# The first matmul of each lot of scores, values and transposes is kept behind everything traced on TensorE ahead of it

## The chip, the core and the metric

The kernel runs on one core of a Trainium2 chip, as one program. The metric is the time of one execution on the device in microseconds. The engines are TensorE (PE; its weight loads are listed apart as PEld), VectorE (DVE), ScalarE (ACT), GpSimd (POOL) and SyncE (SP), which issues the DMAs. Each works through its own list of instructions in order; semaphores hold it where it needs another engine's result.

## The reference

Four batches of 12480 tokens of 128 channels go through an attention over 49 agents, and the result through a feed-forward layer with the activation h cos h.

```python
def sm(a, b):
    s = scale * (a @ b.transpose(0, 2, 1))
    s = s - s.max(-1, keepdims=True)
    e = np.exp(s)
    return e / (e.sum(-1, keepdims=True) + 1e-09)
a2k = sm(agents, k)
agent_v = a2k @ v
q2a = sm(q, agents)
x = (q2a @ agent_v).reshape(B * S, D)
h = x @ w_in
g = h * np.cos(h)
return g @ w_out
```

## The kernel before

Tokens go in 52 groups of 960 (13 for each batch), a group in two halves of 480. For a batch, the agents' values are first multiplied into the 2048 columns of `w_in` (the tiles `a`, and `b1`, `b2` for a correction term), so that a half needs only the 49 weights of each token, turned (`pT`, 113 rows).

The **step loop** (L554) has 832 steps, 8 for each half. A step n multiplies `pT` by two blocks of `a` into `ph` (L562, two matmuls of 480 columns, a *`ph` pair* here), takes the cosine on ScalarE (`c`, L565), and forms (c - 1) h on VectorE (`r`, L567). Four steps later (`LAG`), two matmuls add `r` times `w_out` to the half's output `po` (L584, a *second-layer pair*). With the last step of a half come two correction matmuls (L580, L581) and ScalarE's copy of `po` to `osb` (L586). `ph` has three buffers, each of two PSUM banks.

Between them, by a plan (`plan`, `extra`, L455 to L550), run **lots** that prepare other groups and the next batch. Each stands, in the code, right behind the `ph` pair of its step and ahead of that step's second-layer pair:
- scores of queries or keys (L90): eight matmuls of 49 columns in fp32, each shown as two instructions, so 16 in a lot; then a copy to SBUF on ScalarE (L351, L173) or on VectorE, and a maximum on VectorE (L355, L184);
- values (L235): eight matmuls of 98 columns, 16 instructions; then a sum on VectorE (L240);
- transposes of a group's weights (L380): four; then a copy on ScalarE (`p`, L382), and casts and subtractions on GpSimd that make `pT` (L385, L386).

All lots and the outputs `po` take their PSUM tile from one pool, `one`, of two buffers: `po` holds one, the lots share the other, and when a half ends the two change places. A lot then waits for the copy to `osb` of the half before.

The order on each engine isn't that of the code. A scheduler lays it out ahead of time by its own estimate of when each instruction is ready, the code's order coming second; it may cut a lot into pieces and place them before or behind other pairs. `tc.keep_in_program_order(ins)` adds an edge without a wait: `ins` stays behind the last instruction traced before it on its engine. Before the change it is used for the first loads, for the bursts of exponentials and for one table load. Three times in a batch ScalarE does such a burst, with a table load before and after it.

## Time and profile before

| | |
|---|---|
| median of 3 runs | 1233.39 us (1231.19 to 1235.24) |
| the profiled execution's own time | 1232.16 us |
| its span on the core | 1230.4 us |
| matmuls busy | 1168.4 us |
| VectorE busy | 1074.3 us |
| ScalarE busy | 976.7 us |

Busy times are sums over the span, and the ends of matmuls are modelled, so that TensorE's price for a thing is better read from the distance between starts. What limits a stretch is read from that stretch.

### The profile page before, as it was taken

The page shows a single profiled execution, that of the slowest core. Times are in us where ns is not written, and L with a number is a line of the kernel's source. Part 1 is how long each engine was busy: PE and PEld are TensorE (multiplying, and loading weights), DVE is VectorE, ACT ScalarE, POOL GpSimd, SP SyncE. Part 2 cuts the span into 40 slices and gives each one's busy share as a digit, 9 for nine tenths or more (in the row PEclk, how much of TensorE's full clock was granted, in tenths as well). Part 3 has the DMA queues.
Part 4 walks back from the last instruction along what each step waited for, and adds up shares of the span by engine and source line. Part 5 has one row for each costly group of instructions (what it writes and reads, how often), then busy time and mean ns, then how long its engine had stood idle before and what let it go on. Part 6 is the DMA issues. An engine that isn't in the chain of part 4 may idle for free.

```text
span 1230.4 us, 17371 instructions
## 1 busy us (share of the span) xinstructions
PE 1168.4 (95%) x6349; PEld 963.1 (78%) x6349; DVE 1074.3 (87%) x1219; ACT 976.7 (79%) x1167; POOL 353.1 (29%) x389
## 2 busy tenths in 40 slices
PE   8999999999999999999999999999999999998997
PEld 7878888778887888878787888877878776776674
DVE  5898888988789889898889888888888999999997
ACT  2367788887778888788968888887887888888996
POOL 1211222633322213273412222137332323121220
PEclk9998999999999999999999999999999999998999
DMA  8973232224322232323231232322331110000001
GB/s 310 245 212 97 88 106 80 81 73 136 113 65 81 80 106 71 113 80 103 61 113 61 69 110 80 98 81 81 97 92 38 35 42 37 23 27 27 23 32 35
DMA packets 39190, 107.74 MB, mean 88 GB/s; under 512 B 4344, under 2 KB 4728, under 8 KB 39096
## 3 DMA queue, kind: packets, MB, share of 16 engines
q1 hardware_dynamic: 39096, 106.55, 27.6%
q8 instruction: 52, 0.85, 0.3%
q14 instruction: 42, 0.34, 0.1%
HBM read 80.97 MB, written 25.56 MB: 87 GB/s over the span
## 4 chain that ended last, share of the span: by engine, by line
PE 66%; DVE 16%; ACT 12%; issue 4%; DMA 2%; SPq 0%; ACTq 0%; DVEq 0%
PE ph L562 25%; PE one L584 18%; PE one L90 11%; DVE r L567 10%; ACT c L565 6%; PE one L235 5%; ACT osb L586 3%; PE one L580 2%; PE one L581 2%; DVE rz L364 1%; PE ph L98 1%; DMA raw<-w_out 1%; PE one L380 1%; ACT e L360 1%; DVE mx L355 1%
## 5 line engine op out<-in xcount | busy, mean ns | idle before, releaser
L567 DVE SCALAR_TENSOR_TENSOR r<-c,ph 128x960 fp32r<-128x960 f32 x832 | 923.8, 1149 | 96.1 <-ACT c L565 90.0
L565 ACT ACTIVATE c<-ph 128x960 f32<-128x960 f32 x832 | 795.9, 978 | 176.0 <-PE ph L562 150.3
L562 PE MATMUL ph<-pT,a 113*128 113x480 f32 x1664 | 544.9, 409 | 30.7 <-DVE r L567 21.5
L584 PE MATMUL one<-r,w 128*128 128x480 f32 x1664 | 515.0, 391 | 1.1 <-ACT osb L586 0.6
L562 PEld LDWEIGHTS ph<-pT,a 113*128 113x128 f32 x1664 | 287.1, 192 | 129.8 <-DVE r L567 56.9
L584 PEld LDWEIGHTS one<-r,w 128*128 128x128 f32 x1664 | 311.8, 192 | 47.3 <-ACT osb L586 1.5
L90 PEld LDWEIGHTS one<-ag,xt 128*120 128x120 f32 x1408 | 172.6, 186 | 36.8 <-ACT osb L586 26.0
L371 POOL TENSOR_TENSOR p<-e,rz 120x392 f32<-120x392 f32 x52 | 43.8, 847 | 486.6 <-PE one L380 403.1
L90 PE MATMUL one<-ag,xt 128*120 128x49 f32 x1408 | 172.2, 265 | 9.0 <-ACT osb L586 7.6
L386 POOL TENSOR_TENSOR pT<-p,pT 49x480 fp32r<-49x480 f32 x104 | 126.9, 1220 | 8.0
L385 POOL CAST pT<-p 49x480 fp32r<-49x480 f32 x104 | 60.8, 585 | 74.8 <-ACT p L382 52.4
L235 PEld LDWEIGHTS one<-s,vt 120*128 120x128 f32 x624 | 76.9, 192 | 6.5 <-ACT osb L586 2.6
L357 POOL TENSOR_TENSOR e<-e,mx 120x392 f32<-120x392 f32 x49 | 41.4, 844 | 131.5 <-DVE mx L355 126.3
L235 PE MATMUL one<-s,vt 120*128 120x98 f32 x624 | 77.4, 272 | 1.0 <-ACT osb L586 0.6
L586 ACT COPY osb<-one 128x480 f32<-128x480 f32 x104 | 57.6, 554 | 2.9 <-PE one L584 2.9
L224 POOL TENSOR_TENSOR es<-es,s 120x392 f32<-120x392 f32 x36 | 36.8, 1021 | 47.9 <-ACT s L216 45.6
L380 PEld LDWEIGHTS one<-ident,p 120*113 120x113 f32 x208 | 31.6, 178 | 12.2 <-ACT osb L586 7.2
L580 PE MATMUL one<-pT,b 113*128 113x480 f32 x104 | 41.0, 394 | 0.0
L581 PE MATMUL one<-pT,b 113*128 113x480 f32 x104 | 40.6, 390 | 0.0
L212 POOL TENSOR_TENSOR s<-s,mxb 120x1568 f32<-120x1568 f32 (+1 forms) x9 | 31.6, 3538 | 29.8 <-DVE mxb L208 29.8
L380 PE MATMUL one<-ident,p 120*113 120x120 f32 x208 | 37.4, 274 | 2.3 <-ACT osb L586 2.3
L382 ACT COPY p<-one 113x480 f32<-113x480 f32 x52 | 28.9, 556 | 6.3 <-PE one L380 6.3
(93 smaller groups left out, 532.9 us busy)
## 6 DMA issues: line engine op xcount, KB each, us to landing
xt<-qT SPq DMA_DIRECT2D x52, 480.0 KB, 3.5
vt<-v SPq DMA_DIRECT2D x104, 240.0 KB, 3.5
outT<-osb SPq DMA_DIRECT2D x51, 480.0 KB, 2.6
xt<-kT SPq DMA_DIRECT2D x46, 480.0 KB, 3.5
c<-kT SPq DMA_DIRECT2D x6, 480.0 KB, 5.7
raw<-w_in SPq DMA_DIRECT2D x8, 256.0 KB, 5.3
raw<-w_out SPq DMA_DIRECT2D x8, 256.0 KB, 6.8
outT<-osb SPq DMA_DIRECT2D x2, 240.0 KB, 2.8
```

Source lines behind the costliest of these rows:

```text
L90: nc.tensor.matmul(ps[:, t, :], xt[:, t * TT:(t + 1) * TT], ag[:, b, :], start=True, stop=True)
L235: nc.tensor.matmul(po, vt[:, t, :], twice(e[:, t, :]), start=(t == 0 and (g == 0 or not lone)), stop=(t == GT - 1 and (g == NG - 1 or not ...
L380: nc.tensor.transpose(pt[:KR, t * TT:(t + 1) * TT], p_in[n % 2][:, t, :KR], ident[:TT, :TT])
L385: nc.gpsimd.tensor_copy(pT[own, c], p[own])
L386: nc.gpsimd.tensor_sub(pT[other, c], p[own], pT[own, c].bitcast(F32))
L562: nc.tensor.matmul(ph[:, j, :CH], ai[:, f], pTs[q % 3][:, c], start=True, stop=True)
L565: nc.scalar.activation(cos, h, AF.Sin, bias=HALF_PI, scale=1.0)
L567: nc.vector.scalar_tensor_tensor(r, cos, 1.0, h, op0=ALU.subtract, op1=ALU.mult)
L580: nc.tensor.matmul(po, b1[k], pTs[q % 3][:, c], start=False, stop=False)
L581: nc.tensor.matmul(po, b2[k], pTs[q % 3][:, c], start=False, stop=False)
L584: nc.tensor.matmul(po, w1[:, f, :], r[:, j, :], start=(f == 0), stop=(f == NF - 1))
L586: nc.scalar.copy(osb[:, c * CH:(c + 1) * CH], po)
```

## The change

A list `ordered` switches on a helper `behind` while the step loop is traced. In it, the first matmul of each lot of scores, the first of each lot of values, and the first transpose of each lot is kept behind the last instruction traced on TensorE before it, which is the second matmul of the same step's `ph` pair. The other matmuls of a lot carry no edge.

```diff
--- before.py
+++ after.py
@@ -71,6 +71,12 @@
     fits = const.tile([KR, NB], F32, name="fits")
 
     pinned = [True]
+    ordered = [False]
+
+    def behind(ins):
+        if ordered[0]:
+            tc.keep_in_program_order(ins)
+
 
     def load(dst, src):
         ins = nc.sync.dma_start(dst, src)
@@ -87,7 +93,9 @@
         load(xt, src)
         ps = ps[:TT, :GT * NA].rearrange("p (t a) -> p t a", a=NA)
         for t in range(GT):
-            nc.tensor.matmul(ps[:, t, :], xt[:, t * TT:(t + 1) * TT], ag[:, b, :], start=True, stop=True)
+            mm = nc.tensor.matmul(ps[:, t, :], xt[:, t * TT:(t + 1) * TT], ag[:, b, :], start=True, stop=True)
+            if t in (0,):
+                behind(mm)
         return ps
 
     def scores_twice(xt, src, b, ps):
@@ -232,8 +240,10 @@
                 self.po = self.copies(self.wide()[:, 0] if lone else self.psum())
             e, po = self.part(g), self.po
             for t in range(GT):
-                nc.tensor.matmul(po, vt[:, t, :], twice(e[:, t, :]), start=(t == 0 and (g == 0 or not lone)),
-                                 stop=(t == GT - 1 and (g == NG - 1 or not lone)))
+                mm = nc.tensor.matmul(po, vt[:, t, :], twice(e[:, t, :]), start=(t == 0 and (g == 0 or not lone)),
+                                      stop=(t == GT - 1 and (g == NG - 1 or not lone)))
+                if t in (0,):
+                    behind(mm)
             if g == (NG - 1 if lone else 0):
                 nc.vector.tensor_copy(self.sums, po)
             elif not lone:
@@ -377,7 +387,9 @@
 
             pt = small()
             for t in range(HT):
-                nc.tensor.transpose(pt[:KR, t * TT:(t + 1) * TT], p_in[n % 2][:, t, :KR], ident[:TT, :TT])
+                mm = nc.tensor.transpose(pt[:KR, t * TT:(t + 1) * TT], p_in[n % 2][:, t, :KR], ident[:TT, :TT])
+                if t in (0,):
+                    behind(mm)
             p = sb.tile([KR, CH], F32, name="p")
             nc.scalar.copy(p, pt[:KR, :CH])
             pT = pTs[n % 3]
@@ -551,6 +563,7 @@
 
 
         rs = {}
+        ordered[0] = True
         for n in range(NSTEP + LAG):
             pinned[0] = n < NP
             if n < NSTEP:
@@ -590,6 +603,7 @@
                 elif c == NCH - 1:
                     nc.sync.dma_start(outT[:, at:at + GRP], osb)
         assert not plan.at
+        ordered[0] = False
 
         bx = sb.tile([KR, 1], F32, name="bx", bufs=1)
         nc.vector.tensor_reduce(bx, fits, axis=AX.X, op=ALU.min)
```

No engine gets another instruction. The orders of VectorE and of the DMA queue come out the same as before. On TensorE, at the end of a half in the middle of the loop: the half ends with the tile `one_4079`, the next has `one_4182`, and the lot of key scores is `one_4192` (after the change the lines L90, L235, L380, L562, L584, L580 and L586 are L96, L243, L390, L575, L597, L593 and L599). Before:

```order
L562 MATMUL ph_4154<-pT_0_86,a1_81 128x480 x2
L584 MATMUL one_4079<-r_4121,w1_68 128x480 x2
L562 MATMUL ph_4163<-pT_0_86,a1_81 128x480 x2
L584 MATMUL one_4182<-r_4130,w1_68 128x480 x2
L90 MATMUL one_4192<-ag_65,xt_4193 120x49 x2
L562 MATMUL ph_4175<-pT_0_86,a1_81 128x480 x2
L90 MATMUL one_4192<-ag_65,xt_4193 120x49 x6
L584 MATMUL one_4182<-r_4139,w1_68 128x480
L562 MATMUL ph_4185<-pT_0_86,a1_81 128x480 x2
L584 MATMUL one_4182<-r_4139,w1_68 128x480
L584 MATMUL one_4182<-r_4159,w1_68 128x480 x2
```

And with the change:

```order
L597 MATMUL one_4079<-r_4121,w1_68 128x480
L575 MATMUL ph_4163<-pT_0_86,a1_81 128x480 x2
L597 MATMUL one_4079<-r_4121,w1_68 128x480
L597 MATMUL one_4182<-r_4130,w1_68 128x480 x2
L575 MATMUL ph_4175<-pT_0_86,a1_81 128x480 x2
L597 MATMUL one_4182<-r_4139,w1_68 128x480 x2
L575 MATMUL ph_4185<-pT_0_86,a1_81 128x480 x2
L96 MATMUL one_4192<-ag_65,xt_4193 120x49 x8
L575 MATMUL ph_4207<-pT_0_86,a1_81 128x480 x2
L597 MATMUL one_4182<-r_4159,w1_68 128x480 x2
L597 MATMUL one_4182<-r_4168,w1_68 128x480 x2
L575 MATMUL ph_4216<-pT_0_86,a1_81 128x480 x2
```

The lot was in two pieces around a `ph` pair, right behind the first second-layer pair of the new half; it is in one piece, two `ph` pairs and one second-layer pair later, and the next two second-layer pairs follow each other.

ScalarE's order at the same place, before:

```order
L565 ACTIVATE c_4157<-ph_4154 128x960
L586 COPY osb_4078<-one_4079 128x480
L565 ACTIVATE c_4166<-ph_4163 128x960
L565 ACTIVATE c_4178<-ph_4175 128x960
L173 COPY s_3495<-one_4192 120x392
L565 ACTIVATE c_4188<-ph_4185 128x960
L565 ACTIVATE c_4210<-ph_4207 128x960
```

And with the change:

```order
L578 ACTIVATE c_4166<-ph_4163 128x960
L599 COPY osb_4078<-one_4079 128x480
L578 ACTIVATE c_4178<-ph_4175 128x960
L578 ACTIVATE c_4188<-ph_4185 128x960
L181 COPY s_3495<-one_4192 120x392
L578 ACTIVATE c_4210<-ph_4207 128x960
L578 ACTIVATE c_4219<-ph_4216 128x960
```

The copy out of the lot (to `s_3495`) and the copy to `osb` have each moved behind one more cosine.

A lot of transposes, `one_10849`, in a half late in the loop without other lots, before:

```order
L562 MATMUL ph_10781<-pT_0_86,a1_81 128x480 x2
L584 MATMUL one_10802<-r_10759,w1_68 128x480 x2
L380 MATMUL one_10849<-ident_58,p_1_93 113x120 x2
L562 MATMUL ph_10794<-pT_0_86,a1_81 128x480 x2
L584 MATMUL one_10802<-r_10768,w1_68 128x480 x2
L380 MATMUL one_10849<-ident_58,p_1_93 113x120 x2
L562 MATMUL ph_10805<-pT_0_86,a1_81 128x480 x2
L584 MATMUL one_10802<-r_10777,w1_68 128x480 x2
```

And with the change:

```order
L575 MATMUL ph_10833<-pT_0_86,a1_81 128x480 x2
L597 MATMUL one_10802<-r_10810,w1_68 128x480 x2
L575 MATMUL ph_10842<-pT_0_86,a1_81 128x480 x2
L390 MATMUL one_10849<-ident_58,p_1_93 113x120 x4
L597 MATMUL one_10802<-r_10819,w1_68 128x480 x2
L575 MATMUL ph_10862<-pT_0_86,a1_81 128x480 x2
L593 MATMUL one_10802<-pT_0_86,b11_83 128x480
L594 MATMUL one_10802<-pT_0_86,b21_85 128x480
```

The four transposes stood in two pieces at the half's first pairs; they stand whole, six `ph` pairs later, just ahead of the half's last pairs.

## Rows read from the trace of the kernel before

**Rows 1.** Part 1 of the page: busy time of each engine, its share of the span, and its instructions.
```profile
PE 1168.4 (95%) x6349; PEld 963.1 (78%) x6349; DVE 1074.3 (87%) x1219; ACT 976.7 (79%) x1167; POOL 353.1 (29%) x389
```

**Rows 2.** The waits over the whole span: who waited for whom, us in total, how often, and the longest in us.
```profile
ACT c L565 <- PE ph L562: 150.3, 329, 4.6
...
DVE r L567 <- ACT c L565: 90.0, 220, 1.4
...
PEld ph L562 <- DVE r L567: 56.9, 143, 0.8
...
PEld one L90 <- ACT osb L586: 26.0, 47, 0.6
...
PE one L90 <- ACT osb L586: 7.6, 38, 0.2
PEld one L380 <- ACT osb L586: 7.2, 12, 0.6
...
PEld one L235 <- ACT osb L586: 2.6, 6, 0.6
```

**Rows 3.** The view of busy time by stretch: the stretch, its length, and then of each engine the busy us with its instructions in brackets; last the granted TensorE clock, the DMA share and GB/s. Each stretch is a pair of halves of the step loop with three lots of scores and one of transposes; the first of the 14 such pairs, one of the middle, and the last.
```profile
131.15:152.91 21.76, 21.24 (x122) 17.87 (x121) 19.42 (x21) 17.59 (x23) 5.29 (x6) 1.00 0.25 76
...
476.12:497.99 21.87, 21.18 (x122) 17.99 (x121) 19.15 (x20) 17.82 (x23) 5.28 (x6) 1.00 0.30 91
...
772.76:794.60 21.84, 21.14 (x121) 17.97 (x120) 19.11 (x20) 17.79 (x23) 5.29 (x6) 1.00 0.28 91
```

**Rows 4.** The timeline from 434 to 443.2 us, inside such a pair, of TensorE's matmuls, VectorE and ScalarE: start in us, us, engine, line, operation, tiles, count, and in brackets the idle time before and what ended it.
```profile
434.17 0.59 PE L584 MATMUL one<-r,w 128*128 128x480 f32 x2
...
434.96 0.62 PE L90 MATMUL one<-ag,xt 128*120 128x49 f32 x4 [0.20 <-ACT osb L586]
...
435.40 0.68 PE L562 MATMUL ph<-pT,a 113*128 113x480 f32 x2
...
435.92 1.36 PE L90 MATMUL one<-ag,xt 128*120 128x49 f32 x12
436.11 0.97 ACT L565 ACTIVATE c<-ph 128x960 f32<-128x960 f32 x1 [0.33 <-PE ph L562]
...
437.10 0.69 PE L584 MATMUL one<-r,w 128*128 128x480 f32 x2
437.12 1.15 DVE L567 SCALAR_TENSOR_TENSOR r<-c,ph 128x960 fp32r<-128x960 f32 x1
...
437.31 0.49 ACT L351 COPY e<-one 120x392 f32<-120x392 f32 x1 [0.23 <-PE one L90]
...
437.62 0.60 PE L562 MATMUL ph<-pT,a 113*128 113x480 f32 x2
...
439.26 1.15 DVE L567 SCALAR_TENSOR_TENSOR r<-c,ph 128x960 fp32r<-128x960 f32 x1 [0.99 <-ACT c L565]
...
440.24 0.60 PE L584 MATMUL one<-r,w 128*128 128x480 f32 x2
...
440.33 0.55 DVE L355 TENSOR_REDUCE mx<-e 120x8 f32<-120x392 f32 x1
...
440.81 5.41 DVE L567 SCALAR_TENSOR_TENSOR r<-c,ph 128x960 fp32r<-128x960 f32 x5
...
441.12 0.60 PE L584 MATMUL one<-r,w 128*128 128x480 f32 x2
...
442.00 0.70 PE L562 MATMUL ph<-pT,a 113*128 113x480 f32 x2 [0.29 <-DVE r L567]
...
442.98 0.38 PE L580 MATMUL one<-pT,b 113*128 113x480 f32 x1
...
443.20 0.38 PE L581 MATMUL one<-pT,b 113*128 113x480 f32 x1
```

**Rows 5.** The same view at 529 and 539 us: a lot of transposes and a lot of scores that stand whole with what follows each on TensorE.
```profile
529.52 0.57 PE L380 MATMUL one<-ident,p 120*113 120x120 f32 x4
...
529.86 0.68 PE L584 MATMUL one<-r,w 128*128 128x480 f32 x2
...
538.88 1.78 PE L90 MATMUL one<-ag,xt 128*120 128x49 f32 x16
...
540.48 0.47 PE L584 MATMUL one<-r,w 128*128 128x480 f32 x1
```

**Rows 6.** The view of busy time by stretch for three halves in a row after 980 us: without a lot, with a lot of transposes, without a lot.
```profile
1143.10:1151.88 8.78, 8.57 (x35) 5.91 (x34) 8.61 (x10) 7.92 (x10) 0.00 (x0) 1.00 0.00 0
1151.88:1160.94 9.06, 8.59 (x40) 6.47 (x38) 8.72 (x10) 8.26 (x11) 4.40 (x5) 1.00 0.14 55
1160.94:1169.73 8.79, 8.59 (x36) 5.90 (x34) 8.62 (x10) 7.92 (x10) 0.00 (x0) 1.00 0.01 3
```

**Rows 7.** Part 5 of the page, groups by line: shapes and count, busy us and mean ns of one, and the idle time before them.
```profile
L90 PE MATMUL one<-ag,xt 128*120 128x49 f32 x1408 | 172.2, 265 | 9.0 <-ACT osb L586 7.6
L386 POOL TENSOR_TENSOR pT<-p,pT 49x480 fp32r<-49x480 f32 x104 | 126.9, 1220 | 8.0
L385 POOL CAST pT<-p 49x480 fp32r<-49x480 f32 x104 | 60.8, 585 | 74.8 <-ACT p L382 52.4
...
L382 ACT COPY p<-one 113x480 f32<-113x480 f32 x52 | 28.9, 556 | 6.3 <-PE one L380 6.3
```

## The prediction

> **What bounds the kernel now.** I read the busy shares first, then the waits, then the stretches of the step loop one by one, since the shares are a mean over stages. Matmul is busy 95% of the span, VectorE 87%, weight loads 78%, ScalarE 79% [rows 1]. The waits say who is late: ScalarE's cosine waits for TensorE's `ph` for 150.3 us, VectorE's `r` waits for that cosine for 90.0 us, and TensorE in turn waits for VectorE to free a `ph` buffer and, in 47 + 12 + 6 = 65 places, for ScalarE's `osb` copy to free a `one` buffer ahead of a lot of scores, transposes or values [rows 2].
>
> Two kinds of stretch repeat. In the first, a pair of 8-step halves carries three lots of scores and one of transposes and takes 21.8 to 21.9 us, while VectorE is busy for only 19.1 to 19.4 us of it [rows 3]. There are 14 such pairs: from 131 us on four, from 389 us on five, from 686 us on five. There TensorE is the limit. In the second, after 980 us, a half with no lot takes 8.78 us of which VectorE works 8.61, and eight `r` follow one another without a gap [rows 6]: VectorE is the limit, and nothing done to TensorE's order makes such a half shorter.
>
> **The prices on TensorE** are distances from one start to the next. A `ph` pair or a second-layer pair takes 0.44 us, two of them 0.88, from 440.24 to 441.12 [rows 4]. Each of the two correction matmuls takes 0.22 [rows 4]. A whole lot of scores takes 1.60 us, from 538.88 to 540.48, and a whole lot of transposes 0.34 [rows 5]. The pair behind a lot takes 0.52 in place of 0.44 (437.10 to 437.62 [rows 4]), so I charge 1.68 and 0.42. Twelve and four score matmuls apart take 1.18 and 0.44 [rows 4]: cutting a lot in two makes it neither cheaper nor dearer on TensorE itself.
>
> **The wait that the change removes.** Before, the scheduler starts a lot right behind the first second-layer pair of a new output half. The lot needs the `one` buffer that the old half's `osb` copy is about to free. At 434.17 a second-layer pair starts, and the lot behind it starts at 434.96, 0.79 later in place of 0.44 [rows 4]: 0.35 us lost. In the new order the same lot stands behind two more `ph` pairs and one more second-layer pair, 3 x 0.44 = 1.3 us later, so the copy is over. If all 65 are gone, TensorE gets back 65 x 0.35 = 22.8 us.
>
> What TensorE's rows show of such a wait is an idle time of 0.20 us a piece for the matmul (7.6 us in 38) and 0.55 for the weight load (26.0 in 47) [rows 2]. The Trainium skill says on its page TensorE: Matmul & The Clock Gate, section Step-by-step: what each phase is for, that TensorE pulls weight loads ahead of matmuls in flight. Were that so here, the matmul's own idle time would be the whole price, and the 65 would be worth 13 us by an estimate from it (65 x 0.20); the trace differs, since the loads of the waiting lots wait too, and the 0.35 between starts decides.
>
> **What the change adds.** A lot that stood in two or three pieces between other pairs (as at 434.96 and 435.92 [rows 4]) now stands in one. No instruction is added. VectorE's and the DMA queue's orders stay as they are, ScalarE's moves each copy out of a lot behind the cosine of the step that the lot belongs to, and GpSimd's moves a few subtractions. The danger is VectorE: while the lot runs, no `ph` comes. I laid the new order of one pair out by hand, with the prices above and these: a cosine starts 0.03 behind the end shown for its `ph` pair (435.40 + 0.68, 436.11), so 0.64 behind the start of one that lasts 0.60 (437.62), and takes 0.97; `r` starts 0.03 to 0.04 behind it (436.11 + 0.97, 437.12), takes 1.15, and in a row comes every 1.07 (five in 5.41); a copy out of a lot starts 0.21 behind its last matmul and takes 0.49; a row maximum costs VectorE 0.48 (440.33 to 440.81) [rows 4]. I take the running maximum at the same.
>
> TensorE's work in a pair is 32 x 0.435 + 4 x 0.22 + 3 x 1.68 + 0.42 = 20.26 us. What could hold it up in the new order: the `one` buffer is free 0.4 us ahead of the first lot and 0.6 ahead of the third; every `r` that a second-layer pair reads is over 0.8 us or more before; a `ph` buffer is late twice, behind the running maximum after the first lot (0.11) and behind the transposes (0.18). VectorE's maxima find their copy finished 0.3 to 0.7 us before they get to it, since `r` of the same step stands ahead of them. So a pair takes 20.26 + 0.29 = 20.55 us. VectorE's own need, 19.15 [rows 3], is still below that. Against 21.87 a pair gains 1.32, and 14 pairs gain 18.5 us. Of the 1.32, 0.70 are the two waits for `osb`; the rest is TensorE running ahead and then waiting for a `ph` buffer, as at 442.00, where 0.88 lies between starts in place of 0.44 [rows 4]. The lot now stands where that wait was.
>
> **The other 37 waits.** Thirteen are ahead of transposes in the halves that VectorE limits. Such a half takes 9.06 in place of 8.78 [rows 6], so a wait is worth at most 0.28; in the new order the copy out of the transposes and the `osb` copy come close together on ScalarE, and I take half: 13 x 0.14 = 1.8. The other 24 are in the halves with values, with the bursts of exponentials and in mixed ones; they are worth 0.35 where TensorE is the limit and nothing where the burst is, and I take 0.2: 4.8 us. The queries' transposes come four to six `ph` pairs later, and GpSimd has to make `pT` of them before the next group: behind a lot stand up to one cosine (0.97), the copy (0.56), two casts of 0.585 and two subtractions of 1.22 [rows 7], 5.1 us, of the 7 to 8 that six or seven steps of the new order take, so I charge nothing; without that cover a group would wait for what is missing, under 1 us. Sum: 18.5 + 1.8 + 4.8 = 25.1 us off 1232.2, the profiled execution's own time: 1207. The median of the three runs is 1.2 above that execution, which would make it 1208, and I say 1208.
>
> The bounds: with all pairs at 20.26 (14 x 1.61 = 22.5), all transposes at 0.28 (3.6) and the rest at 0.35 (8.4), 34.5 off: 1198. With the waits for `osb` in the pairs alone (28 x 0.35 = 9.8), 1223.
>
> **Rivals.** *Half of it.* The wait moves along: the `osb` copy itself comes later, because ScalarE's order now puts it behind one more cosine (0.97), or the lot meets another owner of the `one` buffer. My margins of 0.4 to 0.6 us are less than a cosine. Then half of the waits come back in another place: 1220, from 1212 to 1229.
>
> *Nothing, because VectorE is the bound everywhere.* For it: weight loads are busy for 78%, VectorE for 87% [rows 1], and VectorE's order is untouched; TensorE would only wait in other places, and the time would be 1230 to 1236. Against it: in the pairs VectorE is idle for 2.7 of 21.87 us [rows 3] and waits for a cosine that waits for TensorE [rows 2], 0.99 us of it in one piece behind a lot [rows 4]. The Trainium skill's page Perfetto Trace Analysis, section Identifying the Most-Contended Engine, would have it so: TensorE's headroom is judged by the busy share of weight loads and not of matmuls, and by that VectorE is the most contended. The trace agrees for the halves after 980 us and not for the pairs.
>
> *Slower: the whole lot starves VectorE.* The mechanism is the gap at 439.26: behind twelve score matmuls in one piece VectorE was idle for 0.99 us [rows 4]. A whole lot is 0.42 longer (1.60 against 1.18), and of the 88 lots of scores (1408 instructions, 16 in a lot [rows 7]) 16 stand whole in the order before and all 88 in the new one. If VectorE were idle 0.42 longer at each, the loss is 37 us, less the 22.8 of the waits: 14 us slower, 1246. It decides when VectorE has less in hand at a lot's start than the lot, one `ph` pair and a cosine take, 1.68 + 0.44 + 1.2 = 3.3 us; three `ph` buffers hold 3 x 1.07 = 3.2. So VectorE does idle at some lots; the question is whether it makes that up before the next. In my layout it idles 1.4 us in a pair, half of what it does now.
>
> **How the numbers follow.** The forecast has 0.62, half of it 0.15, nothing 0.09, slower 0.14. A measurement of this kernel tells about 0.3% (3.7 us) from no change. Faster by more: 0.62 + 0.15 = 0.77; within: 0.09; slower: 0.14. The range takes in the forecast with its bounds, the half, and the near part of nothing: 1197 to 1233.
>
> **What would show it.** Right: no wait of a lot's first score matmul for the `osb` copy, or a handful; the 14 pairs at 20.4 to 20.8 us; the halves without lots still at 8.78; VectorE's wait for the cosine below 90 us. Wrong: pairs at 21.5 or more with VectorE idle over 1 us behind whole lots (starved); TensorE's wait for `r` or for `pT` grown by more than the wait for `osb` fell; a copy that stands in VectorE's way ahead of a maximum.

## The result and the profile after

The changed kernel takes 1200.61 us in the median (1197.08 to 1205.00, 4 runs) against 1234.32 us before (1231.19 to 1236.82, 4 runs, one more than the table ahead of the prediction had): a ratio of 0.973, with a 95% interval from 0.9688 to 0.9771. The forecast was 1208, the range 1197 to 1233. The profiled execution took 1202.08 us, its span is 1200.3; before, these were 1232.16 and 1230.4.

Part 1 of the page, of the changed kernel, stands against [rows 1]: TensorE does the same matmuls in a shorter span, and the shares of TensorE and VectorE both rise.

```profile
PE 1153.3 (96%) x6349; PEld 970.8 (81%) x6349; DVE 1075.0 (90%) x1219; ACT 968.8 (81%) x1167; POOL 354.7 (30%) x389
```

The waits of the changed kernel, to be laid beside [rows 2] (who waited for whom, us in total, how often, the longest):

```profile
ACT c L578 <- PE ph L575: 99.5, 201, 2.6
PEld ph L575 <- DVE r L580: 56.6, 162, 0.8
DVE r L580 <- ACT c L578: 55.6, 209, 1.2
...
PEld one L597 <- ACT osb L599: 3.1, 4, 0.9
```

No lot of scores (now line 96), values (243) or transposes (390) stands in this list as waiting for the `osb` copy; what is left of that wait is four second-layer pairs and some matmuls outside the lots. The cosine's wait for TensorE fell from 150.3 to 99.5 us, and VectorE's wait for the cosine from 90.0 to 55.6.

Stretches of the changed kernel, in the view of [rows 3] and [rows 6] (start and end, length, busy us of TensorE, weight loads, VectorE, ScalarE and GpSimd with the instructions in brackets, granted clock): one of the pairs of halves with three lots of scores and one of transposes; a half with transposes and the half without a lot behind it; and a half with values behind a burst of exponentials.

```profile
427.00:447.41 20.41, 20.41 (x122) 18.20 (x121) 19.18 (x20) 17.51 (x23) 5.29 (x6) 1.00 0.31 98
...
954.47:964.11 9.64, 9.44 (x41) 6.70 (x40) 9.47 (x10) 8.77 (x11) 0.58 (x1) 1.00 0.13 51
964.11:972.05 7.94, 7.74 (x33) 5.71 (x32) 7.77 (x9) 7.42 (x10) 3.88 (x5) 1.00 0.00 0
589.83:604.32 14.49, 12.85 (x81) 11.22 (x80) 11.12 (x17) 13.54 (x14) 8.95 (x10) 1.00 0.33 102
```

The pair takes 20.41 us in place of 21.87, and in it TensorE's matmuls have no gap: busy for all 20.41 us. The half with transposes and its neighbour take 9.64 + 7.94 = 17.58 in place of 9.06 + 8.78 = 17.84 [rows 6] (the mark between the two moved, so only their sum is compared).

The timeline of the changed kernel around one lot of scores shows how, in the columns of [rows 4]:

```profile
428.94 0.55 ACT L599 COPY osb<-one 128x480 f32<-128x480 f32 x1
...
429.62 0.61 PE L575 MATMUL ph<-pT,a 113*128 113x480 f32 x2
...
430.07 1.78 PE L96 MATMUL one<-ag,xt 128*120 128x49 f32 x16
430.40 2.22 DVE L580 SCALAR_TENSOR_TENSOR r<-c,ph 128x960 fp32r<-128x960 f32 x2 [0.17 <-ACT c L578]
...
431.67 0.67 PE L575 MATMUL ph<-pT,a 113*128 113x480 f32 x2
...
432.18 1.04 PE L597 MATMUL one<-r,w 128*128 128x480 f32 x4
...
432.54 0.55 DVE L365 TENSOR_REDUCE mx<-e 120x8 f32<-120x392 f32 x1
...
433.39 1.16 DVE L580 SCALAR_TENSOR_TENSOR r<-c,ph 128x960 fp32r<-128x960 f32 x1 [0.30 <-ACT c L578]
```

The copy is over at 429.49, 0.58 us ahead of the lot at 430.07. (In the other half of this pair the first lot starts at 439.65, 0.39 us behind its copy, and the halves beside it repeat the two margins.) A `ph` pair stands directly ahead of the lot and another directly behind it, 2.05 us later, and only then do two second-layer pairs follow. VectorE has two `r` and the maximum to do meanwhile and is idle for 0.30 us, where it was idle for 0.99 [rows 4].

### The profile page after: what moved, and what is told of

It is laid out like the page before. It is cut to its first block, busy times and chain, and to the rows that moved or that the text cites. A ratio compares the mean times of both kernels' runs of the same rounds, so it can differ in the third digit from the quotient of the medians.

```text
span 1200.3 us, 17402 instructions
## 1 busy us (share of the span) xinstructions
PE 1153.3 (96%) x6349; PEld 970.8 (81%) x6349; DVE 1075.0 (90%) x1219; ACT 968.8 (81%) x1167; POOL 354.7 (30%) x389
## 4 chain that ended last, share of the span: by engine, by line
PE 70%; DVE 15%; ACT 9%; issue 4%; DMA 1%; SPq 0%; ACTq 0%; DVEq 0%
PE ph L575 25%; PE one L597 21%; DVE r L580 12%; PE one L96 11%; ACT c L578 5%; PE one L243 4%; PE ph L106 2%; PE ph L243 2%; PE one L593 2%; PE one L594 2%; DVE rz L374 2%; PE one L390 1%; ACT osb L599 1%; ACT e L370 1%; DMA vt<-v 1%
## 5 line engine op out<-in xcount | busy, mean ns | idle before, releaser
L580 DVE SCALAR_TENSOR_TENSOR r<-c,ph 128x960 fp32r<-128x960 f32 x832 | 917.4, 1149 | 61.9 <-ACT c L578 55.6
L578 ACT ACTIVATE c<-ph 128x960 f32<-128x960 f32 x832 | 785.5, 979 | 115.5 <-PE ph L575 99.5
L575 PE MATMUL ph<-pT,a 113*128 113x480 f32 x1664 | 537.4, 404 | 26.4 <-DVE r L580 18.5
L597 PE MATMUL one<-r,w 128*128 128x480 f32 x1664 | 497.8, 388 | 2.0 <-ACT osb L599 1.6
L575 PEld LDWEIGHTS ph<-pT,a 113*128 113x128 f32 x1664 | 292.6, 191 | 131.6 <-DVE r L580 56.6
L597 PEld LDWEIGHTS one<-r,w 128*128 128x128 f32 x1664 | 311.3, 191 | 50.6 <-ACT osb L599 3.1
L96 PEld LDWEIGHTS one<-ag,xt 128*120 128x120 f32 x1408 | 161.6, 185 | 7.4 <-DVE e L361 1.7
L96 PE MATMUL one<-ag,xt 128*120 128x49 f32 x1408 | 157.4, 265 | 0.5 <-DVE e L361 0.5
L243 PEld LDWEIGHTS one<-s,vt 120*128 120x128 f32 x624 | 76.0, 192 | 2.5
L243 PE MATMUL one<-s,vt 120*128 120x98 f32 x624 | 75.2, 272 | 0.0
L599 ACT COPY osb<-one 128x480 f32<-128x480 f32 x104 | 57.8, 556 | 2.9 <-PE one L597 2.9
L593 PE MATMUL one<-pT,b 113*128 113x480 f32 x104 | 40.4, 389 | 0.0
L361 ACT COPY e<-one 120x392 f32<-120x392 f32 x40 | 19.5, 488 | 24.2 <-PE one L96 24.2
L181 ACT COPY s<-one 120x392 f32<-120x392 f32 x36 | 17.5, 487 | 21.0 <-PE one L96 21.0
```

The lines of the kernel that those rows point to most:

```text
L96: mm = nc.tensor.matmul(ps[:, t, :], xt[:, t * TT:(t + 1) * TT], ag[:, b, :], start=True, stop=True)
L243: mm = nc.tensor.matmul(po, vt[:, t, :], twice(e[:, t, :]), start=(t == 0 and (g == 0 or not lone)), stop=(t == GT - 1 and (g == NG - 1 or ...
L575: nc.tensor.matmul(ph[:, j, :CH], ai[:, f], pTs[q % 3][:, c], start=True, stop=True)
L578: nc.scalar.activation(cos, h, AF.Sin, bias=HALF_PI, scale=1.0)
L580: nc.vector.scalar_tensor_tensor(r, cos, 1.0, h, op0=ALU.subtract, op1=ALU.mult)
L593: nc.tensor.matmul(po, b1[k], pTs[q % 3][:, c], start=False, stop=False)
```

## The experiments

Three numbers are read from each trace besides the times. *Loop* is the time from the first `ph` pair to the last half's first correction matmul. *Pair* is from the start of the corrections that open one pair of halves to those that open the next, for the two halves that begin near 430 us (three lots of scores, one of transposes). *End* is the same for one half with transposes and one without a lot near 970 us.

| kernel | median us | ratio to before, 95% | loop | pair | end |
|---|---|---|---|---|---|
| before | 1234.32 | | 1146.6 | 21.87 | 17.84 |
| changed | 1200.61 | 0.973 (0.9688 to 0.9771) | 1109.6 | 20.41 | 17.58 |
| e1 scores alone | 1204.84 | 0.9772 (0.9742 to 0.9801) | 1116.7 | 20.71 | 17.84 |
| e2 without values | 1197.37 | 0.9717 (0.9681 to 0.9752) | 1109.2 | 20.39 | 17.57 |
| e3 later | 1207.01 | 0.9781 (0.975 to 0.9813) | 1120.3 | 21.07 | 17.79 |
| e4 all in traced order | 1228.55 | 0.9953 (0.9927 to 0.9979) | 1138.9 | 21.02 | 17.16 |
| e5 second layer behind a lot | 1216.69 | 0.9853 (0.9812 to 0.9894) | 1131.1 | 21.04 | 17.58 |
| e6 cut, same place | 1210.42 | 0.981 (0.9771 to 0.9848) | 1123.0 | 21.20 | 17.58 |
| e7 cut, moved | 1218.90 | 0.9886 (0.9841 to 0.9931) | 1129.0 | 20.87 | 17.83 |
| e8 corrections too | 1198.09 | 0.9713 (0.9672 to 0.9754) | 1108.0 | 20.87 | 17.21 |
| e9 late copy | 1218.69 | 0.9859 (0.9822 to 0.9897) | 1130.8 | 21.73 | 17.36 |
| e10 end in traced order | 1192.60 | 0.9672 (0.9638 to 0.9707) | 1104.4 | 20.40 | 17.15 |
| e11 corrections in places | 1192.03 | 0.9648 (0.9617 to 0.9679) | 1101.3 | 20.41 | 17.18 |
| e12 the same without values | 1193.99 | 0.9666 (0.9637 to 0.9694) | 1100.9 | 20.40 | 17.18 |

Each ratio is to runs of the kernel before that were taken together with the kernel in its row. Pairs and ends repeat to some hundredths of a us where two kernels have the same order there (pairs of 20.39 to 20.41 in five kernels). Halves with a burst do not: TensorE's order in the first 74 halves of e10 is that of the changed kernel, and they take 831.7 us against 834.2, with single halves apart by up to 0.9. What lies ahead of the loop varies still more, and the last section shows how. So mechanisms are read from pairs and ends, loops of one execution each are compared to some 2.5 us, and versions by the ratios.

**e1: scores alone.** The pin stays in `scores` and is taken out of `values` and `query_turned`:

```diff
-                if t in (0,):
-                    behind(mm)
             if g == (NG - 1 if lone else 0):
...
-                if t in (0,):
-                    behind(mm)
             p = sb.tile([KR, CH], F32, name="p")
```

> Only the lots of scores are kept back; values and transposes stand as before. Theory (the gain is the wait of lots for the osb copy, plus TensorE running ahead and then standing in front of a ph buffer, mostly at the lots of scores): the 14 pairs keep their 1.46 us each (20.4 us), the 13 transposes in halves limited by VectorE lose 0.26 each (3.4 us) and the values up to 2: 1203 to 1207 us. Rival (the gain is that lots are no longer cut into pieces): 72 of the 116 lots that were cut are whole, the rest stays cut, so about 62% of the gain of 33.7 us: 1213 us.

A pair of this kernel in the view by stretch:

```profile
422.36:443.06 20.70, 20.66 (x121) 18.11 (x120) 19.35 (x20) 17.55 (x23) 5.29 (x6) 1.00 0.30 96
```

1204.84, inside the theory's 1203 to 1207 and far from the rival's 1213. One detail missed: the pairs are not at 20.4 but at 20.70. The transposes in them stand where the scheduler puts them again, and TensorE's weight loads then wait for a `ph` buffer for 0.6 us in two places of such a pair, in place of 0.2 in one. The 14 pairs lose 3.9 us and the last 26 halves, where transposes wait again, 3.1; together that is the 7.1 us by which the loop is longer.

**e2: without values.** The pin is taken out of `values` alone.

> Scores and transposes are kept back, values stand as before. Theory: values waited for an osb copy in 6 places, 2.6 us in all, so at most 3 us slower than the changed kernel: 1200 to 1204 us; if the two halves that became 1.1 us longer each in the changed kernel became so through the values that were kept back, 2 us faster: 1198 to 1199. Rival (cutting): 9 lots of values are cut again, under 3 us: the same.

1197.37 lies below both of the theory's ranges and is the rival's "the same": a loop of 1109.2 against 1109.6, no difference that can be told. In sum the pin of values gives nothing and costs nothing that these runs could show; single halves gain or lose by it up to 1.4 us (16.83 in place of 15.44 in one with values, 12.92 in place of 13.83 in the one behind it).

**e3: later.** The lots are traced behind the second-layer pair of their step, not ahead of it:

```diff
-            plan.run(n)
             m = n - LAG
...
+            plan.run(n)
             if i == NP - 1:
```

> All three kinds are kept back, but the lots are traced behind the second-layer pair of their step. In the order lots then stand three ph pairs and three second-layer pairs behind the corrections, as in the changed kernel, but 48 of 92 lots of scores, 14 of 55 of transposes are cut again. VectorE's order is the same. Theory (the wait): no waits for osb, 1199 to 1204 us. Rival (wholeness): half of the lots are cut again, so half of the gain is lost: 1215 us.

A pair of this kernel in the view by stretch:

```profile
430.58:451.65 21.07, 20.92 (x122) 18.20 (x121) 18.84 (x19) 17.61 (x23) 5.23 (x6) 1.00 0.30 94
```

1207.01 is above the theory's range and below the rival's 1215. No lot of scores waits for `osb` here either, and yet the pair takes 21.07: 0.80 less than before, 0.66 more than the changed kernel. So the waits are not the whole gain. A second-layer pair now stands ahead of a lot, and it is 2.48 us from one `ph` pair over a whole lot to the next, in place of 2.05; but half of the lots are also cut in this kernel, so it leaves open whether the rest comes from wholeness or from what stands next to a lot; e4 to e7 go after that.

**e4: all in traced order.** Every `ph`, correction and second-layer matmul gets the pin too:

```diff
-                    nc.tensor.matmul(ph[:, j, :CH], ai[:, f], pTs[q % 3][:, c], start=True, stop=True)
+                    behind(nc.tensor.matmul(ph[:, j, :CH], ai[:, f], pTs[q % 3][:, c], start=True, stop=True))
```

and likewise for the two corrections and the second layer.

> Every matmul of the step loop is kept in the order it was traced, not only the first one of a lot. All lots are whole, but 58 of them stand two ph pairs and two second-layer pairs behind the corrections, where they stood before the change. Theory (the wait): the waits for the osb copy are back, some 50 to 65 of 0.35 us and the run-ahead that follows them: 1217 to 1234 us. Rival (wholeness): 1197 to 1205 us, as the changed kernel.

The stretches of this kernel, a pair, a half with transposes and one without a lot; then three stretches of 3 us each in a half with values:

```profile
437.88:458.90 21.02, 20.89 (x122) 18.12 (x120) 18.89 (x19) 17.26 (x23) 5.28 (x6) 1.00 0.30 94
985.27:993.88 8.61, 8.60 (x39) 6.46 (x38) 8.61 (x9) 8.22 (x11) 1.34 (x2) 1.00 0.14 57
...
615.00:618.00 3.00, 1.20 (x5) 0.41 (x4) 3.00 (x6) 2.62 (x4) 1.76 (x2) 1.00 0.66 182
618.00:621.00 3.00, 1.52 (x7) 1.52 (x8) 3.00 (x5) 0.36 (x1) 0.00 (x0) 0.76 0.02 5
621.00:624.00 3.00, 3.00 (x14) 2.86 (x14) 0.57 (x3) 0.00 (x0) 0.00 (x0) 0.50 0.00 0
```

The time of 1228.55 lies where the theory put it, but for another reason, and the expectation was set wrongly: it counted the distance from the corrections, and in this order the old half's last second-layer pair follows them at once, where it stood behind one more `ph` pair before. So the old half ends one pair sooner, a lot comes three pairs behind that end in place of two, and waits for no `osb` copy. The loss in the pairs (21.02 against 20.41) has to come from elsewhere, with all lots whole; a second-layer pair follows each lot here, as in e5 below. The pairs lose 9.2 us of the loop's 29.3. 8.1 more are lost in the first four halves, where the granted clock is 0.64 from 78 to 102 us, and most of the rest around the bursts. There, in three halves, a pinned lot of values waits for VectorE's sum of values (`av`, 2.5 us at the longest) and everything behind it waits too: from 615 to 621 us TensorE is busy for 2.72 of 6 us, and then the granted clock falls to 0.50. What this kernel does better is the end: 17.16 in place of 17.58, with VectorE busy all the time.

**e5: second layer behind a lot.** In the changed kernel a lot of scores stands as `ph`, lot, `ph`, second layer. Here it is `ph`, lot, second layer, `ph`: in a step with a lot of scores the second-layer pair is pinned, and so is the next `ph` pair.

```diff
+                    if j == 0 and behind_lot[0]:
+                        behind(mm)
+                        behind_lot[0] = False
...
+                if j == 0 and behind_lot[0]:
+                    behind(mm)
```

> As the changed kernel, but behind each lot of scores one second-layer pair is kept ahead of the next ph pair (ph, lot, second layer, ph in place of ph, lot, ph, second layer). Lots are whole and no lot stands nearer to the osb copy. Theory (part of the gain beyond the waits for osb comes from the ph pair that now stands directly behind a lot, so that VectorE is fed 0.44 us sooner): the 14 pairs go from 20.40 to about 21.0 us, as in the run with every matmul in traced order (21.02), so the step loop from its first ph pair to its last correction goes from 1109.6 to 1118 us and the time to about 1209. Rival (wholeness alone, with the waits gone): pairs stay at 20.40 and the time at 1200.

The timeline of this kernel around a lot (97 is the scores' line, 577 `ph`, 602 the second layer, 585 `r`):

```profile
434.43 0.59 PE L577 MATMUL ph<-pT,a 113*128 113x480 f32 x2
434.86 1.78 PE L97 MATMUL one<-ag,xt 128*120 128x49 f32 x16
436.47 0.68 PE L602 MATMUL one<-r,w 128*128 128x480 f32 x2
...
436.99 0.60 PE L577 MATMUL ph<-pT,a 113*128 113x480 f32 x2
...
438.63 2.22 DVE L585 SCALAR_TENSOR_TENSOR r<-c,ph 128x960 fp32r<-128x960 f32 x2 [0.73 <-ACT c L583]
...
449.29 0.38 PE L602 MATMUL one<-r,w 128*128 128x480 f32 x1
449.73 0.70 PE L577 MATMUL ph<-pT,a 113*128 113x480 f32 x2
```

And of this pair's waits:

```profile
PEld ph L577 <- DVE r L585: 1.0, 2, 0.5
```

From one `ph` pair to the next it is 2.56 us in place of 2.05, and VectorE is idle for 0.73 us behind the lot in place of 0.30. The pair takes 21.04, as the theory said: lots whole, no wait for `osb`, and 0.63 us lost by the second-layer pairs that stand between a lot and the next `ph` pair. Wholeness alone is ruled out. On TensorE the 0.63 are two waits for a `ph` buffer: at 449.73 a `ph` pair starts 0.44 behind a single second-layer matmul in place of 0.22, and its second matmul another 0.10 late; with a like wait 5.5 us earlier that makes 0.66. The loop lost more than the pairs do (21.5 us in all, 10.1 in the 14 pairs); the pins also hold up the first four halves (6.7 us in all) and the last two of the first two groups of 26 (4.2 and 2.6), which the expectation had left out; 1216.69 was measured where 1209 was expected.

**e6 and e7: cut lots.** Both queue the first four matmuls of a lot behind the `ph` pair of the step before and the last four behind that of its own step. e7 also traces lots one step later in a half.

```diff
+            with ExitStack() as queue:
+                if ordered[0]:
+                    queue.enter_context(tc.issue_after(last_ph[-2:][0 if t < GT // 2 else -1].ins))
...
-            while n in taken or (n - LAG) % NP not in ((1, 2, 3, 4, 5) if dense else (1, 3, 5)):
+            while n in taken or (n - LAG) % NP not in ((1, 2, 3, 4, 5) if dense else (2, 4, 6)):
```

(the last two lines in e7 alone).

> As the changed kernel, with ScalarE's, VectorE's and the DMA queue's orders equal to it, but most lots of scores are cut four and four matmuls around a ph pair (second layer, 4 scores, ph, 4 scores, second layer, ph). The first piece comes one ph pair nearer to the osb copy than in the changed kernel, where the margin was worked out at 0.4 us, so no wait or under 0.1 us each. Theory (what stands behind a lot decides): a second-layer pair stands between each second piece and the next ph pair, so the 14 pairs take about 21.0 us and the loop 1118 us. Rival (what decides is the longest time without a ph pair, which is halved): 20.4 us and 1110. Second rival (wholeness): 21.2 us or more.

> Lots of scores are cut four and four, each piece directly behind a ph pair, with a second-layer pair behind each piece, and lots are traced one step later in a half (2, 4, 6 in place of 1, 3, 5), so that no piece is near the osb copy. Theory (what stands behind a lot decides): pairs at 20.7 to 21.0 us. Rival (longest time without a ph pair decides): a piece, a second-layer pair and a ph pair take 0.84 + 0.44 + 0.44 = 1.7 us against 2.1 in the changed kernel, so pairs at TensorE's own 20.3 to 20.4 us. Second rival (wholeness): 21.2 us or more.

The wait in e6, where 100 is the scores' line, and TensorE's timeline at two places of a pair (600 is the second layer, 577 `ph`):

```profile
PEld one L100 <- ACT osb L602: 12.0, 32, 0.4
```

```profile
426.85 0.60 PE L600 MATMUL one<-r,w 128*128 128x480 f32 x2
...
427.43 1.04 PE L100 MATMUL one<-ag,xt 128*120 128x49 f32 x8
...
432.28 0.60 PE L600 MATMUL one<-r,w 128*128 128x480 f32 x2
...
432.95 0.71 PE L577 MATMUL ph<-pT,a 113*128 113x480 f32 x2
```

In e6 a small wait is back, by the starts 0.14 us each (0.58 from 426.85 to 427.43 in place of 0.44) and two of them in a pair, and the pair takes 21.20, which is also the second rival's value. Of the 0.79 above the changed kernel 0.28 are these waits; 0.33 are a wait for a `ph` buffer at 432.95 (0.23, and 0.10 more ahead of its second matmul); 0.18 are left for three cuts. Without the waits for `osb` it would be 20.92 by that estimate, no longer than with whole lots and a second-layer pair behind (21.04), so wholeness is worth little. The first rival wanted 20.4: from one `ph` pair to the next it is 1.88 us at most here, less than the 2.05 of the changed kernel, and a wait for a `ph` buffer is there all the same. But two such stretches follow each other (1.88 and 1.80), which the rival had not thought of.

In e7 each piece has a `ph` pair ahead and a second-layer pair behind; 20.87 is in the theory's range, but by another wait:

```profile
434.04 0.60 PE L577 MATMUL ph<-pT,a 113*128 113x480 f32 x2
...
434.85 0.71 PE L600 MATMUL one<-r,w 128*128 128x480 f32 x2 [0.21 <-ACT p L396]
```

Traced one step later, the transposes stand so near to the end of a half that the first second-layer pair of the next half waits for the copy `p` to free its `one` buffer: 0.81 us lie between the starts in place of 0.44, and its second matmul is 0.11 late. These 0.48 are all of the 0.46 by which the pair is longer than the changed kernel's, and no `ph` pair in it starts late, with at most 1.74 us from one to the next. Without that wait the pair would be near 20.4 by this estimate, which is the rival's value. So e7 does not decide between the theory and the rival by which the longest time without a `ph` pair counts. e7 is slow in all (1218.90) mostly because of its bursts: the two halves from 210 us on take 30.55 in place of 25.31.

**e8: corrections too.** The changed kernel, and the first correction matmul of every half is pinned:

```diff
-                nc.tensor.matmul(po, b1[k], pTs[q % 3][:, c], start=False, stop=False)
+                behind(nc.tensor.matmul(po, b1[k], pTs[q % 3][:, c], start=False, stop=False))
```

> As the changed kernel, and the first of the two correction matmuls at a half's end is kept behind everything traced ahead of it, so that a ph pair no longer waits behind the corrections. In the run with every matmul in traced order the halves without lots take 8.55 us and those with transposes 8.60, in place of 17.58 for the two in the changed kernel, and VectorE has no gap there. Theory (ph pairs late behind the corrections): the halves without scores in the last quarter go from 17.58 to 17.15 a pair of them, 8 to 10 such pairs in the whole loop: 4 us off, about 1197 us, loop 1105. Rival (VectorE limits them anyhow): 17.58 and 1200. The pairs with scores stay at 20.4.

What it is aimed at is seen in the timeline of the changed kernel at the start of a half:

```profile
972.05 0.38 PE L593 MATMUL one<-pT,b 113*128 113x480 f32 x1
972.27 0.37 PE L594 MATMUL one<-pT,b 113*128 113x480 f32 x1
972.48 0.60 PE L575 MATMUL ph<-pT,a 113*128 113x480 f32 x2
...
975.45 1.16 DVE L580 SCALAR_TENSOR_TENSOR r<-c,ph 128x960 fp32r<-128x960 f32 x1 [0.17 <-ACT c L578]
```

The corrections (0.43 us) stand ahead of a `ph` pair, and at 975.45, behind a row of `r` without a gap, VectorE has been idle for 0.17. With the pin the `ph` pair goes first, and the two halves take 17.21 in place of 17.58: VectorE no longer waits there. That half of the expectation came true. The other did not: the pairs went from 20.41 to 20.87. The scheduler, which now ends a half in another place, puts a second-layer matmul between one of the three lots and the next `ph` pair, as in e5, and TensorE waits once in a pair for a `ph` buffer (0.5 us by the starts); that the one follows from the other is argued from the order. So the loop is shorter by 1.6 us where 4 were expected, which is no more than the same order varies.

**e9: late copy.** The changed kernel, with the `osb` copy kept behind one more cosine:

```diff
+            while late:
+                late.pop()()
             plan.run(n)
...
-                nc.scalar.copy(osb[:, c * CH:(c + 1) * CH], po)
+                def out(osb=osb, po=po, q=q, c=c):
+                    tc.keep_in_program_order(nc.scalar.copy(osb[:, c * CH:(c + 1) * CH], po))
```

> As the changed kernel, but the osb copy is kept behind one more cosine on ScalarE, so it ends 1.07 us later; the scheduler, which sees that, puts one second-layer pair or one half of it (0.44 or 0.22 us) ahead of the first lot of a half. Theory (a lot that finds its one buffer taken holds TensorE up for what is missing): the copy is later by 1.07, the lot by 0.22 to 0.44, the margin of the changed kernel was worked out at 0.4, so about 0.3 us of wait a lot is back, two in a pair: 20.40 + 2 x 0.3, and one second-layer pair more behind which nothing changes: pairs at about 21.0, TensorE's waits of lots for osb at 15 us or more, 1110 + 9 in the loop, 1210 in all. Rival (the waits for osb cost nothing of themselves, all of the gain is in what stands beside a lot): pairs at 20.4 to 20.5 and 1201 to 1203.

Its waits, and its timeline around a lot:

```profile
PEld one L96 <- ACT osb L602: 25.5, 46, 0.8
...
PE one L96 <- ACT osb L602: 7.7, 37, 0.4
```

```profile
439.98 0.59 PE L575 MATMUL ph<-pT,a 113*128 113x480 f32 x2
440.39 0.55 ACT L602 COPY osb<-one 128x480 f32<-128x480 f32 x1
440.41 0.39 PE L599 MATMUL one<-r,w 128*128 128x480 f32 x1
...
440.99 1.88 PE L96 MATMUL one<-ag,xt 128*120 128x49 f32 x16 [0.20 <-ACT osb L602]
...
442.69 0.68 PE L575 MATMUL ph<-pT,a 113*128 113x480 f32 x2
```

The wait is back as it was: 25.5 and 7.7 us against 26.0 and 7.6 in [rows 2], with 440.99 - 440.41 - 0.22 = 0.36 us between starts. 21.2 us of the loop are lost and the time is 1218.69, where 1210 was expected; the rival (the waits cost nothing) is out. The pair takes 21.73, 1.32 more than the changed kernel's where 0.6 were expected. By the starts 0.73 of it are the two waits; about 0.2 are inside the two waiting lots, which take 1.70 us to the next pair in place of 1.60; about 0.4 are `ph` pairs that find no buffer free, since a second-layer matmul and the wait make it 2.71 us from one `ph` pair to the next in place of 2.05. Of such a wait the row of the matmul shows 0.20. The Trainium skill (TensorE: Matmul & The Clock Gate, Step-by-step: what each phase is for) says that weight loads are pulled ahead of matmuls in flight; here the loads of the waiting lot wait as well (25.5 us), and 46 waits at 0.20 would make 9 us of the 21.

**e10 to e12: versions.** The three put together what was found. e10 is the changed kernel with everything in traced order, but from step 596 on alone, where mostly transposes are left. e11 pins the first correction, but only at the ends of halves in which e8 had gained; e12 is e11 without the pin of values.

```diff
+            tight[0] = n >= 596
...
+                if any(x <= m // NP < y for x, y in ((13, 22), (39, 48), (65, 74), (77, 104))):
+                    behind(mm)
```

(the first line in e10, with a pin on each matmul of the step while `tight` holds; the other two in e11 and e12, on the first correction).

> The changed kernel, and from step 596 on, where mostly transposes are left, every matmul in the order it was traced. Theory (there VectorE is held up by ph pairs that stand behind the corrections, and in traced order it is not): the last 26 halves take 231.4 us as in the run with everything in traced order, in place of 237.6, the first 74 halves as in the changed kernel: step loop 1103 to 1104 us, the time 6 us below the changed kernel, about 1194. Rival (a gain there is given back at the border): 1200.

> The changed kernel, and the first correction matmul kept behind everything traced ahead of it, but only at the ends of the halves 13 to 21, 39 to 47, 65 to 73 and 77 to 103, where the run that kept it everywhere gained. Theory: 3.3 us in the halves 14 to 21, 2.1 in 40 to 47, 2.2 in 66 to 73 and 6.8 in the last 26: step loop 1095 us, the time about 1186. Rival (these gains came with the halves beside them and do not add up): loop 1103 to 1108, the time 1194 to 1198.

> As the run with the corrections kept back in some halves, but lots of values are not kept back. Theory (a lot of values that waits for VectorE's running sum or GpSimd holds up what stands behind it; unpinned, other work passes it): 0 to 3 us faster than with them: 1183 to 1186. Rival (values start too early again and wait for osb, 3 us in all): 1187 to 1190.

Stretches of e10, a half with transposes and one without a lot:

```profile
949.45:958.03 8.58, 8.56 (x39) 6.45 (x38) 8.58 (x9) 8.15 (x11) 1.33 (x2) 1.00 0.14 57
958.03:966.59 8.56, 8.54 (x35) 5.93 (x34) 8.56 (x9) 8.13 (x10) 3.14 (x4) 1.00 0.00 0
```

VectorE is busy for the whole of both, so nothing on TensorE can shorten them. e10 hits the numbers that were expected, a loop of 1104.4 and 1192.60 us, in part by luck. The last 26 halves (counted from 0: 78 to 103) take 231.6 us in place of 237.6, as expected; but the four halves ahead of them, where the traced order begins, take 41.1 in place of 37.9, so that from half 74 on the gain is 2.8 in all and not 6.0, as the rival had it in part (the granted clock is 0.87 in one of the four); and the first 74, whose order is the same, happened to take 2.4 less. e11 falls short: its loop is 1101.3 where 1095 were expected. Inside the four ranges the gains add up (3.3 us in the halves 14 to 21, 2.0 in 40 to 47, 2.9 in 66 to 73), but the two halves ahead of each range lose 1.9, 1.2, 1.1 and 1.7, 5.9 us in all. Why is open: the pin may begin one half too early, and the pinned correction is also the mark that tells halves apart, so that part of such a gain is only taken from the half ahead. To begin it one half later was not tried. e12 is the same as e11 (1193.99 and 1192.03, the intervals overlap) and misses both of the ranges that were set for it. e11 is faster than the changed kernel, since its interval lies below that one's; e10's interval overlaps with it.

## Why the prediction was right, and where its sizes were off

**The wait that was removed.** Right: all of the 65 places are gone, and the price was right. Measured from the second-layer matmul ahead of a lot to the lot, whatever is over the usual 0.22, the kernel before lost 23.4 us in 67 places, 0.35 in most of them, where 22.8 was the price of all 65. e9 shows that this time is really lost: when the wait is put back, the loop is 21.2 us longer, 17.4 of it read in the same way in 51 places. The margins between the copy and the lot were worked out at 0.4 and 0.6 us and measured at 0.39 and 0.58.

**The pairs.** 1.32 us each were expected, 0.70 of it from the two waits, the rest from TensorE running ahead and then waiting for a `ph` buffer; a typical pair gained 1.46. The starts bear this out. In the pair before, the two lots start 0.35 and 0.36 us late, and the `ph` pair at 442.00 0.44 late, with another 0.10 ahead of its second matmul [rows 4]: 1.25 of the 1.46; the rest is hundredths that belong to no single place. In the changed pair no start is late except for the 0.08 or 0.09 ahead of the second matmul of the pair behind each lot, which the prediction had charged. So 20.41 is TensorE's own work, and what the pairs of the other kernels take beyond it is what TensorE waits for in them: a `ph` buffer in e5, `osb` copies and a `ph` buffer in e6 and e9, the copy `p` in e7.

e5 splits the gain by experiment: 21.87 to 21.04 with the waits for `osb` gone (0.83), and 21.04 to 20.41 with the `ph` pair directly behind the lot (0.63). With whole lots a pair was the longer, the later that next `ph` pair starts behind the last one: 2.05 us in the changed kernel, 2.56 in e5, 2.71 in e9, where the waits for `osb` add to it. Whether a lot that is cut would do as well was not settled: e6 and e7 have shorter distances than 2.05, and both have waits of their own.

The prediction's 20.55 was near for two errors against each other: its own work of 20.26 was 0.15 too small, and the 0.29 of late `ph` buffers did not come. The 14 pairs gained 18.2 us against 18.5, and that is partly luck too: eleven came out at 20.4 to 20.7, the very first with a gain of 1.01 and the others with about 1.46, but the first of each of the other two groups gained 0.35 and the last of the first group 1.89.

**The transposes at the end.** 0.14 was expected for a wait there, half of the bound 0.28; a half with transposes and its neighbour gained 0.27 (17.84 to 17.58), so the bound was the right value. All 26 halves from 980 us on gained 4.1 us where 1.8 was expected. (The thirteen waits there are ten of transposes and three of scores; [rows 2] has twelve of transposes in the whole kernel.) The statement that these halves are VectorE's and that nothing in TensorE's order can shorten a half without lots was wrong: 8.78 was not VectorE's limit. e4, e8 and e10 bring them to 8.55 to 8.61, eight `r` of 1.07, by letting a `ph` pair go ahead of the corrections. "VectorE busy 8.61 of 8.78" [rows 6] held 0.17 us of waiting, so the eight `r` did not follow one another without a gap.

**The other 24 waits** are the term that was mis-sized: 4.8 us expected. The loop gained 37.0; less 18.2 for the pairs and 4.1 for the halves from 980 us on, 14.7 remain, nearly all of it in halves with values, bursts and mixed lots. They were priced at 0.2 each, but by the starts most of them held TensorE up for 0.35; and a pair of halves gained more than its waits alone, as the pure ones did: the mixed pairs 1.40 us each (the two that begin at 498 and 795 us before), those with a burst or values anything from -0.7 to 1.8. Part of that may be TensorE's clock. The half with values and the one behind it, in the kernel before, by stretch:

```profile
602.23:618.62 16.39, 14.41 (x83) 12.20 (x82) 12.74 (x20) 14.37 (x14) 5.11 (x5) 0.93 0.31 90
618.62:633.25 14.63, 14.63 (x91) 13.37 (x90) 11.59 (x14) 9.24 (x12) 1.33 (x2) 0.96 0.44 136
```

Before, the granted clock was 0.93 and 0.96 there; in the changed kernel it is 1.00 in the first (589.83 to 604.32, above), and the two together take 28.60 in place of 31.03. Summed over the loop, half by half, the length times what the clock lacks of 1.00 falls from 18.6 to 13.6 us. So the clock explains about 5 of the 14.7 us at most, by an estimate from one execution of each kernel; no run held the order and changed the clock alone, so how the 14.7 divide stays open.

**The sum.** Expected 25.1 off, measured 33.7 in the medians and 37.0 in the loop. The loops are of one execution each. The profiled ones are 30.1 apart, because in that of the changed kernel the first `ph` pair starts at 82.4 us in place of 76.0, with the same work ahead of it (below); the medians probably hold executions of either kind.

**The rivals.** *Half of it* did not happen: counted from the start of the half's last second-layer pair, the copy starts 1.06 us later before (434.35 - 433.29) and 1.07 after (428.94 - 427.87). e9 is what it would have been. *Nothing, VectorE is the bound everywhere*: in the pair TensorE's matmuls are busy 20.41 of 20.41 us, VectorE 19.18. The Trainium skill (Perfetto Trace Analysis, Identifying the Most-Contended Engine) would judge TensorE by its weight loads (or by its arithmetic rate, which is not read here), 18.20, and name VectorE; the order of TensorE alone took 1.46 us off this pair, so here the matmuls are the measure. *Slower, the whole lot starves VectorE*: its mechanism exists, and e5 shows it (idle 0.73 us), but it hangs on what stands behind the lot more than on the lot's length: with the `ph` pair next, VectorE is idle for 0.30 us behind a whole lot and had been for 0.99 behind a cut one.

GpSimd's `pT` for the next group, which was charged nothing, cost nothing: no `ph` pair waits for it in the list of waits.

## What to carry to other kernels

Where one engine feeds another through a few buffers, place a long piece of other work with a feeding step directly ahead of it and directly behind it, and let everything that can be late go after that. Here a second-layer pair ahead of that next step cost 0.63 us in a pair of halves; whether cutting the piece up would do as well stays open. A scheduler that starts work when its model says a buffer is free will hit the engine's wait each time the model is a few tenths of a us early, and a single order edge on the first instruction cured it here; pinning everything gave little (1228.55 us), since behind a pinned instruction whose operand is late the whole engine stands. To see what an order costs, read the distances between starts: the changed pair and the one before differ by 1.46 us, and the busy share of matmuls shows half of that as idle. Before calling a stretch bound by an engine that is busy 98% of it, look for the one gap that recurs, and which instruction on the feeding engine stood in front.

## What was not expected of the hardware

The time ahead of the loop changes between executions though the work there is the same in all these kernels. In 14 profiled executions the first `ph` pair starts at 74.7 to 77.8 us in nine, and at 82.1 to 84.2 in five; in those five TensorE's granted clock in the stretch from 40 to 60 us is 0.50 to 0.57, in the other nine 1.00. The changed kernel is one of the five:

```profile
38.00:40.00 2.00, 0.81 (x7) 0.81 (x8) 2.00 (x6) 1.77 (x4) 0.00 (x0) 1.00 0.99 257
40.00:42.00 2.00, 2.00 (x16) 2.00 (x16) 2.00 (x5) 1.78 (x4) 0.00 (x0) 0.75 0.56 152
...
56.00:58.00 2.00, 2.00 (x11) 2.00 (x11) 0.00 (x0) 0.00 (x0) 0.00 (x0) 0.50 0.82 244
```

and the same stretch of the kernel before:

```profile
38.00:40.00 2.00, 0.56 (x5) 0.32 (x4) 2.00 (x6) 1.24 (x3) 0.00 (x0) 1.00 1.00 251
40.00:42.00 2.00, 2.00 (x18) 2.00 (x19) 2.00 (x6) 1.78 (x4) 0.00 (x0) 1.00 0.95 246
```

TensorE stands still for over half of the two us ahead, in both (busy 0.81 and 0.56 of 2.00); in one the clock then falls to 0.50, its lower level of 1.2 GHz, for some 17 us, in all of which TensorE is busy, in the other it stays at 2.4 GHz. The cost is about 7 us of 1200, by where the loop starts, more than several of the differences that were sought here. What decides between the two was not found. In e4 the clock falls too, between 618 and 624 us, behind a stretch in which TensorE was busy for 2.72 of 6 us.
